# Experts in pairs of 512 tokens, the first layer in seven block products held in PSUM

## The chip, the cores and the metric

The kernel runs on one core of one Trainium2 chip. The metric is the device time of one execution in microseconds (us), and the figure of a kernel is the median of its runs. Engines are named as the profile names them: PE is TensorE's matrix multiplication and PEld its weight load, DVE is VectorE, ACT is ScalarE, POOL is GpSimd, SP is SyncE, which issues most of the DMAs.

## The reference, cut to what matters

The first part mixes each sequence by a Fourier transform; the second sends every token to one of 8 experts, a two-layer network with a relu between.

```python
batch, seq, dim = (8, 2496, 256)
N, D, E, F = (19968, 256, 8, 1024)
...
    X = np.fft.rfft(x, axis=1)
    Yr = Xr @ w_r - Xi @ w_i + b_r
    Yi = Xr @ w_i + Xi @ w_r + b_i
    Yr = np.sign(Yr) * np.maximum(np.abs(Yr) - lam, 0.0)
    Yi = np.sign(Yi) * np.maximum(np.abs(Yi) - lam, 0.0)
    y = np.fft.irfft(Y, n=x.shape[1], axis=1)
...
    logits = x @ w_gate + modality_bias[modality_id]
    e_idx = np.argmax(logits, axis=1)
    gate_w = probs[np.arange(N), e_idx]
    for e in range(E):
        mask = e_idx == e
        h = np.maximum(x[mask] @ w1[e], 0.0)
        out[mask] = gate_w[mask, None] * (h @ w2[e])
```

The experts are very unevenly used: of the 19,968 tokens of these inputs 9,993 go to expert 2 and 9,756 to expert 6.

## The kernel before

**The attention part** (0 to 627 us of the trace) works through the 8 sequences one after the other. Each has a stage of transforms and mixing, a stage of inverse products (`zs`, line 358), and then a "pivot" stage of 22 steps `j` (lines 372 to 387), in which PE multiplies, ACT and DVE split each result in a high and a low part, and the finished tokens are scattered by POOL into the DRAM tensor `xs`, sorted by expert. Routing, and a table of token tiles per expert, are made beside it. At some of the steps `j` a `SplitWeights.step` takes one 128x512 block of the experts' weights, splits it in a high (ACT, line 1070) and a low part (DVE or POOL, line 1071) and writes both to the DRAM tensor `wsp`. The order of the instructions on PE, ACT, DVE and POOL is the order in which the code emits them; SP issues its DMAs in that order too and waits at each for what it needs.

**The expert part** (627 to 1510 us) runs 78 tiles of 256 tokens (`NF`, `T`), sorted by expert; the table says the first row and the expert of each. Every number is a high and a low fp32r part, and every product three matmuls (high x high, high x low, low x high). For a tile, `ffn` does:
- first layer (line 829): 48 matmuls of 128x256, in four PSUM banks of a pool of four (`mhps`), each bank two of the 8 blocks of 128 hidden columns. A bank is then read twice: ACT writes `hh` = relu, 128x512 (line 831), DVE the low part `hl` (line 832);
- second layer (line 859): 48 matmuls into one bank `y` (two halves of 128 tokens x 256), all of them after the tile's first layer;
- output: half 0 is multiplied by the gate on ACT (line 851), half 1 on DVE (line 849), and POOL writes each with an indirect DMA (`put`, line 872).

Between the second and the third bank of a tile `prep` makes the next tile ready: DVE transposes (line 803), ACT casts the high part (line 807), POOL subtracts the low part (line 808). The weights have two buffers. `load_w` (line 771) loads 2 MB for each layer and tile, and only if the expert has changed; the first layer's load for tile i+2 is issued in the middle of tile i, the second layer's behind tile i. `load_x` (line 789) is issued four tiles ahead, in 8 DMAs of 32 KB and a small one for gates and indices. Between groups of matmuls `tick` lets the last sequence's routing, the second table and the scatters go on; `pack` and `half` compute the few tokens of the small remainders.

The code works only with blocks as they are stored: a weight `w1` of an expert is 256 x 1024, two blocks of 128 rows.

## Time and profile before

| | us |
|---|---|
| median of 3 runs (range) | 1517.15 (1514.96 to 1519.22) |
| profiled execution, device time | 1518.66 |
| its span in the trace | 1516.9 |
| PE busy | 1455.8 (96%) |
| DVE busy | 720.6 (48%) |
| ACT busy | 648.1 (43%) |
| POOL busy | 499.8 (33%) |
| mean granted clock of PE | 0.985 of full speed |

All rows below are of this one profiled execution. A row of a timeline gives the start, the length (of a run of xcount like instructions), the engine, the line of the kernel and "out<-in"; in brackets stands how long the engine was idle before it and what released it. Matmuls overlap: the length of one contains a pipeline that the next one shares, so the rate is read from the distance of starts. The columns of a group are busy time in us, mean ns of one, idle time just before them, and what ended most of that.

### The profile page before, as it was taken

The page shows a single profiled execution, that of the slowest core. Times are in us where ns is not written, and L with a number is a line of the kernel's source. Part 1 is how long each engine was busy: PE and PEld are TensorE (multiplying, and loading weights), DVE is VectorE, ACT ScalarE, POOL GpSimd, SP SyncE. Part 2 cuts the span into 40 slices and gives each one's busy share as a digit, 9 for nine tenths or more (in the row PEclk, how much of TensorE's full clock was granted, in tenths as well). Part 3 has the DMA queues.
Part 4 walks back from the last instruction along what each step waited for, and adds up shares of the span by engine and source line. Part 5 has one row for each costly group of instructions (what it writes and reads, how often), then busy time and mean ns, then how long its engine had stood idle before and what let it go on. Part 6 is the DMA issues. An engine that isn't in the chain of part 4 may idle for free. (4 is left out here: it accounts for less than half of the span.)

```text
span 1516.9 us, 34943 instructions
## 1 busy us (share of the span) xinstructions
PE 1455.8 (96%) x12378; PEld 1400.1 (92%) x12378; DVE 720.6 (48%) x1553; ACT 648.1 (43%) x1360; POOL 499.8 (33%) x501
## 2 busy tenths in 40 slices
PE   4799999999999988999999999999999999899998
PEld 2699999999999887999999999999999999899998
DVE  3667767677676664554333333333333333233332
ACT  3367677776767553532323323322322333232322
POOL 0001344444444453333643232222322323223222
PEclk8899999999999998999999999999999999999999
DMA  7858787979786655422442255642522227525520
GB/s 200 260 149 271 219 292 232 309 222 310 230 290 207 209 186 144 159 47 56 98 121 52 52 134 146 224 128 44 170 43 45 54 46 265 158 51 161 161 43 30
DMA packets 289702, 235.80 MB, mean 155 GB/s; under 512 B 208304, under 2 KB 243452, under 8 KB 285785
## 3 DMA queue, kind: packets, MB, share of 16 engines
q1 hardware_dynamic: 270677, 191.95, 44.4%
q0 software_dynamic: 18848, 41.58, 8.3%
q8 instruction: 100, 1.64, 0.5%
q14 instruction: 77, 0.63, 0.1%
HBM read 424.05 MB, written 99.68 MB: 345 GB/s over the span
## 5 line engine op out<-in xcount | busy, mean ns | idle before, releaser
L859 PE MATMUL y<-w,hh 128*128 128x256 f32 x2496 | 434.5, 277 | 1.1 <-ACT hh L831 1.0
L829 PE MATMUL h<-xh,w 128*128 128x256 f32 x2496 | 400.4, 277 | 4.3 <-DMA w<-wsp 3.3
L859 PEld LDWEIGHTS y<-w,hh 128*128 128x128 f32 x2496 | 377.4, 188 | 3.6 <-issue 1.7
L859 PE MATMUL y<-w,hl 128*128 128x256 f32 x1248 | 347.1, 278 | 0.6 <-DVE hl L832 0.4
L829 PEld LDWEIGHTS h<-xh,w 128*128 128x128 f32 x2496 | 337.3, 188 | 5.1 <-issue 3.9
L832 DVE SCALAR_TENSOR_TENSOR hl<-h,hh 128x512 fp32r<-128x512 f32 x312 | 209.2, 689 | 228.7 <-ACT hh L831 185.5
L872 POOL DMA_INDIRECT out<-o,ix x157 | 154.8, 986 | 419.2 <-ACT o L851 386.1
L829 PE MATMUL h<-xl,w 128*128 128x256 f32 x1248 | 244.2, 277 | 0.0
L831 ACT ACTIVATE hh<-h 128x512 fp32r<-128x512 f32 x312 | 178.1, 596 | 147.0 <-PE h L829 128.1
L859 PEld LDWEIGHTS y<-w,hl 128*128 128x128 f32 x1248 | 234.2, 188 | 2.0 <-DVE hl L832 1.7
L849 DVE TENSOR_SCALAR o<-y,xt 128x256 f32<-128x256 f32 x78 | 37.7, 484 | 328.3 <-ACT o L851 324.2
L829 PEld LDWEIGHTS h<-xl,w 128*128 128x128 f32 x1248 | 188.5, 188 | 0.2 <-DVE xl L808 0.2
L851 ACT ACTIVATE o<-y,xt 128x256 f32<-128x256 f32 x78 | 37.1, 476 | 351.5 <-PE y L859 351.5
L808 POOL TENSOR_TENSOR xl<-tr,xh 128x512 fp32r<-128x512 f32 x76 | 98.5, 1296 | 181.8 <-ACT xh L807 181.8
L547 POOL DMA_INDIRECT xs<-x1b,si x88 | 88.2, 1002 | 84.2 <-ACT ph L377 31.3
L372 PE MATMUL pv<-pv,z 128*120 128x136 f32 x704 | 111.8, 284 | 1.6 <-DVE mid L454 0.9
L547 POOL DMA_INDIRECT xs<-x,si x88 | 88.0, 1000 | 69.1 <-ACT ph L377 28.8
L334 PE MATMUL mx<-wmix,Xh 128*128 128x256 f32 x640 | 105.5, 288 | 3.5 <-DVE mx L327 3.1
L372 PEld LDWEIGHTS pv<-pv,z 128*120 128x120 f32 x704 | 100.1, 187 | 8.4 <-ACT z L362 2.2
L378 DVE TENSOR_TENSOR pl<-pv,ph 120x264 fp32r<-120x264 f32 x176 | 75.8, 431 | 64.4 <-ACT ph L377 52.2
L807 ACT CAST xh<-tr 128x512 fp32r<-128x512 f32 x78 | 48.4, 621 | 107.3 <-DVE ix L810 86.4
L303 PE MATMUL s<-c_m,a 128*128 128x128 f32 x640 | 86.1, 278 | 7.7 <-DMA a<-scr 7.7
(211 smaller groups left out, 2023.6 us busy)
## 6 DMA issues: line engine op xcount, KB each, us to landing
w<-wsp SPq DMA_DIRECT2D x156, 2048.0 KB
a<-scr SPq DMA_DIRECT2D x80, 256.0 KB
xt<-xs SPq DMA_DIRECT2D x624, 32.0 KB
wr<-in_moe_w SPq DMA_DIRECT2D x64, 256.0 KB
wsp<-wh SPq DMA_DIRECT2D x64, 256.0 KB
wsp<-wl SPq DMA_DIRECT2D x64, 256.0 KB
scr<-ev SPq DMA_DIRECT2D x98, 160.0 KB
x<-in_x SPq DMA_DIRECT2D x96, 156.0 KB
```

The lines of the kernel that those rows point to most:

```text
L303: nc.tensor.matmul(ps[:, c, :, i, :], at[:, i, c * 128:(c + 1) * 128], self.m[:, k1 * 128:(k1 + 1) * 128].rearrange("p (r k) -> p r k", r= ...
L334: self.nc.tensor.matmul(ps[:, i, :], t[:, c, 1 - i, :], self.w[:, i, c, lo, :], start=False, stop=n == len(ops) - 1, skip_group_check=True)
L372: nc.tensor.matmul(ps[:PK, c * 128:c * 128 + D // 2 + E], self.z[:, o:o + 3, :, :].rearrange("p n k r -> p (n k r)"), self.pv[:, c, :], st ...
L378: nc.vector.tensor_sub(pl, ps[:PK, :GC], ph)
L547: i = self.nc.gpsimd.indirect_dma_start(out=self.xs, out_offset=bass.IndirectOffsetOnAxis(ap=si[:, k:k + 1], axis=0), in_=rows, in_offset= ...
L807: nc.scalar.copy(xh, tr)
L808: (nc.gpsimd if i > 1 else nc.vector).tensor_sub(xl, tr, xh)
L829: nc.tensor.matmul(ps[:, q, :], w1[:, lo, c, f * 128:(f + 1) * 128], x[:, c, :], start=n == 0, stop=n == 5)
L831: nc.scalar.activation(hh[:, 2 * p:2 * p + 2, :], ps, AF.Relu)
L832: nc.vector.scalar_tensor_tensor(hl[:, 2 * p:2 * p + 2, :], ps, 0.0, hh[:, 2 * p:2 * p + 2, :], ALU.max, ALU.subtract)
L859: nc.tensor.matmul(y[s], lhsT, w2[:, lo, f, :], start=n == 0, stop=n == 23)
L872: ins = self.nc.gpsimd.indirect_dma_start(out=self.out, out_offset=bass.IndirectOffsetOnAxis(ap=ix, axis=0), in_=o, in_offset=None, bounds ...
```

## The change

**Units and pairs.** The table now gives first 32 pairs of 512 tokens (`PAIRS`, `T2`), then 14 single tiles of 256 (46 `SLOTS`). Each is done in four units U = 4i + f; unit f makes the 128 hidden columns f of each half of the 1024 hidden ones. `second(U - 2)` is a generator with the second layer of the unit two back, and pieces of it are emitted between the products of unit U. `y` takes two banks for a pair, one for each 256 tokens, and is added up over the four units.

**Seven products.** In pairs 7 to 31 (`LEAD` is 7) a unit has the form 2x2 blocks times 2x2 blocks: two 128-row blocks of x by two groups of 256 tokens, and two row blocks by two hidden halves of `w1`. Eight block products become seven, each of 3 matmuls of 128x256, with sums and differences of blocks. The sums of weights are the new `w3` (1.5 MB per expert, loaded by `load_s`), the sums of x the new `df`. Three PSUM banks hold the running block sums r1, r5 and r2: ACT copies r1 to the bank of r2 (both in PSUM), copies r5 and r2 to `s5` and `su2` in SBUF, and PE goes on adding to r1, r2 and r5 meanwhile; DVE adds them into `d`, a bank of the routing pool. Pairs 0 to 6 and the singles (`plain`) take eight products as before.

**Weights.** In the attention part `sum` adds two blocks of `w1` before they are split, at step j two before the `step` that writes them; a `step` now writes one DMA of 512 KB instead of two of 256 KB. In the expert part `combos`, advanced by each `tick` from unit 4 on, reads `w1` again, makes the three sums per expert, splits them and writes them to the DRAM tensor `wss` (8 MB read, 12 MB written).

**The rest.** x is loaded two slots ahead in 8 DMAs of 64 KB per pair. In pairs 7 to 31 all four output multiplications are on ACT. `pack` and `half` move behind the pairs, into the singles.

```diff
+T2 = 2 * T
+EARLY = -(-(NTOK - 2 * SEQ - E * (T2 - 1)) // T2)
+PAIRS = -(-(NTOK - E * (T2 - 1)) // T2)
+SLOTS = PAIRS + NF - 2 * PAIRS
+LEAD = 7
...
+        def low_parts():
+            if two:
+                split(0, b[0])
+                split(T, tr[:, 1, :])
+                yield
+                split(3 * T, df[:, 0, :])
+                yield
+                split(5 * T, df[:, 1, :])
+                return
...
+        if two:
+            V.tensor_sub(d[0], b[1], b[0])
+            V.tensor_sub(d[1], b[3], b[1])
+            yield
+            V.tensor_sub(d[2], b[3], d[0])
+            V.tensor_sub(d[3], b[2], d[2])
...
+    def plain(self, U, i, f, second):
+
+        n = self.size(i)
+        if n == T:
+            ps = self.bank().tile([128, 2, T], F32, tag="h", name=f"h_{U}")
+            for q, parts in enumerate((((0, 0), (1, n)), ((3, 0), (2, 2 * n)))):
+                self.mm(ps[:, q, :], self.terms(i, parts, f, 0, T))
+                next(second, None)
+                self.tick()
+            self.drain(U, slice(0, 2), slice(0, T), ps)
+            return
+        for q, parts in enumerate((((0, 0), (1, n)), ((3, 0), (2, 2 * n)))):
+            ps = self.bank().tile([128, T2], F32, tag="h", name=f"h_{U}_{q}")
+            for t in range(0, n, T):
+                self.mm(ps[:, t:t + T], self.terms(i, parts, f, t, T))
+            self.drain(U, q, slice(0, n), ps[:, :n])
+            for _ in range(2):
+                self.tick()
+                next(second, None)
+
+    def strassen(self, U, i, f, second):
+
+        nc, V = self.nc, self.nc.vector
+        xh, xl = self.xs[i][:2]
+        w1, w3, fs = self.wb[i % 2][0], self.w3[i % 2], slice(f * 128, (f + 1) * 128)
+        r1, r5, r2 = (self.hps[n].tile([128, T2], F32, tag="h", name=f"r{k}_{U}")[:, T:]
+                      for n, k in enumerate((1, 5, 2)))
+
+        def prod(ps, w, k, o, start):
+            o = slice(o * T, (o + 1) * T)
+            self.mm(ps, [(w[:, k, lo, fs], x[:, o]) for lo, x in ((0, xh), (0, xl), (1, xh))], start)
+
+        tmp = lambda tag: self.sp.tile([128, T], F32, tag=tag, name=f"{tag}_{U}")
+        a, b = slice(0, T), slice(T, T2)
+        s5, su2 = tmp("s5"), tmp("su2")
+        d = self.rt.ps.tile([128, 2, T], F32, tag="r", name=f"d_{U}")
+        hh, hl = self.hs[U]
+        next(self.next, None)
+        prod(r1, w1, 0, 0, True)
+        nc.scalar.copy(r2, r1)
+        prod(r5, w1, 3, 3, True)
+        nc.scalar.copy(s5, r5)
+        next(second, None)
+        prod(r2, w3, 0, 5, False)
+        nc.scalar.copy(su2, r2)
+        prod(r1, w1, 1, 1, False)
+        self.drain(U, 0, a, r1)
+        if f:
+            next(self.splits, None)
+        next(second, None)
+        self.tick()
+        prod(r2, w3, 1, 4, False)
+        V.tensor_add(d[:, 1, :], r2, s5)
+        prod(r5, w3, 2, 2, False)
+        V.tensor_add(d[:, 0, :], r5, su2)
+        self.drain(U, slice(0, 2), b, d)
+        next(second, None)
+        self.tick()
+        prod(r2, w1, 2, 6, False)
+        self.drain(U, 1, a, r2)
+        next(second, None)
+
...
+    def second(self, U):
...
+                c = 4 * q + f
+                a, l = hh[:, q, s * 128:(s + 1) * 128], hl[:, q, s * 128:(s + 1) * 128]
+                for x, lo in ((a, 0), (a, 1), (l, 0)):
+                    nc.tensor.matmul(y, x, w2[:, c // 2, lo, c % 2, :], start=f == 0 and k == 0 and s % 2 == 0,
+                                     stop=f == 3 and k == 5, skip_group_check=True)
+                    k += 1
+            if f == 3 and s % 2:
+                o = self.op.tile([128, 2, D], F32, tag="o", name=f"o_{i}_{s}")
+                for h in range(2):
+                    gate = g[:, s - 1 + h, 0:1]
+                    if h and not LEAD <= i < PAIRS:
+                        nc.vector.tensor_scalar_mul(o[:, h, :], self.y[i][s // 2][:, h, :], gate)
+                    else:
+                        nc.scalar.mul(o[:, h, :], self.y[i][s // 2][:, h, :], gate)
+                    self.put(ix[:, s - 1 + h:s + h], o[:, h, :])
+            yield
...
+        load(0)
+        for e in range(E):
+            load(e + 1)
+            yield
+            raw = raws.pop(e)
+            a11, a21, a12, a22 = (raw[:, c, h * 512:(h + 1) * 512] for c in range(2) for h in range(2))
+            V.tensor_add(a22, a21, a22)
+            yield
+            V.tensor_sub(a21, a11, a21)
+            yield
+            V.tensor_sub(a22, a22, a11)
+            yield
+            V.tensor_sub(a12, a12, a22)
+            yield
+            for k, a in enumerate((a22, a21, a12)):
+                w = wp.tile([128, 2, 512], F32R, tag="wt", name=f"ws_{e}_{k}")
+                nc.scalar.copy(w[:, 0, :], a)
+                V.tensor_sub(w[:, 1, :], a, w[:, 0, :])
+                nc.sync.dma_start(self.wss[e * 128:(e + 1) * 128, k * 1024:(k + 1) * 1024],
+                                  w.rearrange("p h f -> p (h f)").bitcast(F32))
+                yield
...
+        with ExitStack() as lead:
+            self.blocks(range(4))
+            self.more = self.combos(lead)
+            self.blocks(range(4, 4 * LEAD - 4))
+            for _ in self.more:
+                pass
+        with ExitStack() as mid:
+            w3 = self.pool("mw3", 1, mid)
+            self.w3 = [w3.tile([128, 3, 2, 512], F32R, name=f"w3_{i}") for i in range(2)]
+            self.sp = self.pool("mst", 1, mid)
+            for i in (LEAD, LEAD + 1):
+                self.load_s(i)
+            self.blocks(range(4 * LEAD - 4, 4 * PAIRS))
...
+        for U in units:
+            i, f = divmod(U, 4)
+            second = self.second(U - 2) if U >= 2 else iter(())
+            if i < SLOTS:
+                self.hs[U] = tuple(self.hp.tile([128, 2, T2], F32R, tag=t, name=f"{t}_{U}") for t in ("hh", "hl"))
+                if f == 0:
+                    self.next = self.prep(i + 1) if i + 1 < SLOTS else iter(())
+                if LEAD <= i < PAIRS:
+                    self.strassen(U, i, f, second)
+                else:
+                    next(self.next, None)
+                    self.plain(U, i, f, second)
+                    if f:
+                        next(self.splits, None)
...
+                            self.load_s(i + 2)
+            for _ in second:
+                pass
+            if f == 1 and 0 < i < SLOTS - 1:
+                self.load_w(i + 1, 1)
...
+    def sum(self, eng):
+
+        if self.raw and self.raw[0][1] == 1:
+            raw = self.raw[0][2]
+            for h in range(2):
+                eng.tensor_add(raw, raw, self.last[:, h, :])
...
+                    at_j = (3, 8, 13, 18) if b in (0, nb - 2) else (4, 10, 15)
+                    if j + 2 in at_j:
+                        sw.sum(nc.vector)
+                    if j in at_j:
                         sw.step(nc.vector)
```

PE, tile 39 of before, start of its second bank (`h_39_1`): one run of 12 matmuls, with a wait on PE's own record of the bank, and so for each bank.

```order
L829 MATMUL h_39_1_14800<-xh_39_14657,w1_1_8497 128x256 [waits PE_49]
L829 MATMUL h_39_1_14800<-xh_39_14657,w1_1_8497 128x256
L829 MATMUL h_39_1_14800<-xl_39_14658,w1_1_8497 128x256 x2
L829 MATMUL h_39_1_14800<-xh_39_14657,w1_1_8497 128x256 x4
L829 MATMUL h_39_1_14800<-xl_39_14658,w1_1_8497 128x256 x2
L829 MATMUL h_39_1_14800<-xh_39_14657,w1_1_8497 128x256 x2
```

PE, unit 29 (second unit of pair 7) of after: `r5` and `r2` are two of its running sums, `w1_1` and `w3_1` the weights and their sums, `y_6_0` an output bank of pair 6.

```order
L899 MATMUL r5_29_10890<-xh_7_10496,w1_1_8403 128x256 [waits DVE_49]
L899 MATMUL r5_29_10890<-xl_7_10497,w1_1_8403 128x256
L899 MATMUL r5_29_10890<-xh_7_10496,w1_1_8403 128x256
L983 MATMUL y_6_0_10664<-w2_0_8368,hh_27_10742 128x256 x2
L983 MATMUL y_6_0_10664<-w2_0_8368,hl_27_10743 128x256
L983 MATMUL y_6_0_10664<-w2_0_8368,hh_27_10742 128x256 x2
L983 MATMUL y_6_0_10664<-w2_0_8368,hl_27_10743 128x256
L899 MATMUL r2_29_10891<-xh_7_10496,w3_1_10462 128x256 [waits Activation_49]
L899 MATMUL r2_29_10891<-xl_7_10497,w3_1_10462 128x256
L899 MATMUL r2_29_10891<-xh_7_10496,w3_1_10462 128x256
L899 MATMUL r1_29_10889<-xh_7_10496,w1_1_8403 128x256
```

Between r1 and the first addition onto r2 now stand r5's three matmuls and six of the second layer, and that addition waits for ACT.

ACT, tile 3 of before: four relus, one cast for the next tile, one output multiplication.

```order
L831 ACTIVATE hh_3_9113<-h_3_0_9115 128x512 [waits PE_49,Activation_49]
L831 ACTIVATE hh_3_9113<-h_3_1_9132 128x512 [waits PE_49]
L807 CAST xh_4_9151<-tr_4_9149 128x512 [waits DVE_49]
L831 ACTIVATE hh_3_9113<-h_3_2_9157 128x512 [waits PE_49]
L831 ACTIVATE hh_3_9113<-h_3_3_9173 128x512 [waits PE_49]
L851 ACTIVATE o_3_9197<-y_3_9196,xt_3_8572 128x256 [waits DMAHW3_49,PE_49]
L831 ACTIVATE hh_4_9276<-h_4_0_9278 128x512 [waits PE_49,Activation_49]
```

ACT, unit 61 of after (the second unit of pair 15), with the outputs `o_14` of the pair before and the casts `xh_16` of the pair behind.

```order
L944 COPY r2_61_13443<-r1_61_13441 128x256 [waits PE_49]
L946 COPY s5_61_13444<-r5_61_13442 128x256 [waits PE_49,Activation_49]
L949 COPY su2_61_13445<-r2_61_13443 128x256 [waits PE_49,Activation_49]
L894 ACTIVATE hh_61_13439<-r1_61_13441 128x256 [waits PE_49]
L850 CAST xh_16_13381<-tr_16_13361 128x256 [waits Pool_49]
L850 CAST xh_16_13381<-tr_16_13361 128x512
L993 ACTIVATE o_14_1_13482<-y_14_0_13227,g_14_12095 128x256 [waits DMASW3_49,DMAHW4_49,DMASW2_49,PE_49]
L993 ACTIVATE o_14_1_13482<-y_14_0_13227,g_14_12095 128x256
L894 ACTIVATE hh_61_13439<-d_61_13446 128x2x256 [waits DVE_49]
L894 ACTIVATE hh_61_13439<-r2_61_13443 128x256 [waits PE_49]
L993 ACTIVATE o_14_3_13518<-y_14_1_13228,g_14_12095 128x256 [waits DMASW5_49,DMASW4_49,PE_49]
L993 ACTIVATE o_14_3_13518<-y_14_1_13228,g_14_12095 128x256
```

The copies, which didn't exist, stand ahead of the relus, and two casts and four multiplications stand between them and the next unit's copy `r2_62<-r1_62`.

DVE, pivot stage of the first sequence, before: `pl` is the low part that the next inverse product takes, `x1l` a split for a later sequence, line 1071 a weight split.

```order
L378 TENSOR_TENSOR pl_0_7_1184<-pv_0_7_1180,ph_0_7_1183 120x264 [waits PE_49,Activation_49]
L251 TENSOR_TENSOR x1l_2_9_1188<-x_2_4_842,x1h_2_9_1187 117x512 [waits Activation_49]
L378 TENSOR_TENSOR pl_0_8_1208<-pv_0_8_1204,ph_0_8_1207 120x264 [waits PE_49,Activation_49]
L387 COPY x1b_108<-i1_0_6_1211 117x264
L1071 TENSOR_TENSOR wl_0_1_1217<-wr_0_1_959,wh_0_1_1216 128x512 [waits Activation_49]
L378 TENSOR_TENSOR pl_0_9_1228<-pv_0_9_1224,ph_0_9_1227 120x264 [waits PE_49,Activation_49]
```

DVE, the same stage, after.

```order
L384 TENSOR_TENSOR pl_0_6_1171<-pv_0_6_1167,ph_0_6_1170 120x264 [waits PE_49,Activation_49]
L393 COPY x1b_109<-i1_0_4_1174 117x264
L1276 TENSOR_TENSOR wr_0_1_960<-wr_0_1_960,wt_0_3_1119 128x512
L1276 TENSOR_TENSOR wr_0_1_960<-wr_0_1_960,wt_0_3_1119 128x512 [waits DVE_49]
L384 TENSOR_TENSOR pl_0_7_1185<-pv_0_7_1181,ph_0_7_1184 120x264 [waits PE_49,Activation_49]
L257 TENSOR_TENSOR x1l_2_9_1189<-x_2_4_843,x1h_2_9_1188 117x512 [waits Activation_49]
```

Between two of the `pl` (line 378 before, 384 after) stand two additions onto the raw weight block `wr_0_1`, the second of which waits for the first.

## Rows read from the trace of the kernel before

**Rows 1.** The page's engine totals: busy us, share of the span, instructions.

```profile
PE 1455.8 (96%) x12378; PEld 1400.1 (92%) x12378; DVE 720.6 (48%) x1553; ACT 648.1 (43%) x1360; POOL 499.8 (33%) x501
```

**Rows 2.** Expert stage: length, busy of PE, PEld, DVE, ACT, POOL, clock, DMA.

```profile
627.20:1509.80 882.60, 877.25 (x7646) 868.79 (x7646) 314.40 (x643) 261.79 (x479) 275.65 (x256) 1.00 0.40 105
```

**Rows 3.** Groups by line, both layers: busy, mean ns, idle before, releasers.

```profile
L829 PE MATMUL h<-xh,w 128*128 128x256 f32 x2496 | 400.4, 277 | 4.3 <-DMA w<-wsp 3.3 <-ACT xh L807 1.0
L859 PE MATMUL y<-w,hh 128*128 128x256 f32 x2496 | 434.5, 277 | 1.1 <-ACT hh L831 1.0 <-DMA w<-wsp 0.2
```

**Rows 4.** TensorE's timeline where six tiles begin: start, us, instruction, [idle, releaser].

```profile
627.22 0.62 PE L829 MATMUL h<-xh,w 128*128 128x256 f32 x3 [0.99 <-ACT xh L807]
...
662.60 0.40 PE L829 MATMUL h<-xh,w 128*128 128x256 f32 x2
...
673.91 0.40 PE L829 MATMUL h<-xh,w 128*128 128x256 f32 x2
...
797.68 0.40 PE L829 MATMUL h<-xh,w 128*128 128x256 f32 x2
...
1208.84 0.39 PE L829 MATMUL h<-xh,w 128*128 128x256 f32 x2
...
1219.72 0.40 PE L829 MATMUL h<-xh,w 128*128 128x256 f32 x2
```

**Rows 5.** TensorE's timeline where weights came late.

```profile
1300.27 0.47 PE L829 MATMUL h<-xh,w 128*128 128x256 f32 x2 [3.32 <-DMA w<-wsp]
1300.59 0.40 PE L829 MATMUL h<-xl,w 128*128 128x256 f32 x2
...
1306.95 0.47 PE L859 MATMUL y<-w,hh 128*128 128x256 f32 x2 [0.98 <-ACT hh L831]
```

**Rows 6.** Timelines of PE and ACT, then groups: PSUM reads of 256 and 512.

```profile
1208.72 0.28 PE L859 MATMUL y<-w,hl 128*128 128x256 f32 x1
...
1209.04 0.48 ACT L851 ACTIVATE o<-y,xt 128x256 f32<-128x256 f32 x1 [4.59 <-PE y L859]
...
612.53 0.38 ACT L387 COPY x<-i 117x264 f32<-117x264 f32 x1
612.80 0.40 ACT L377 CAST ph<-pv 120x264 fp32r<-120x264 f32 x1
...
L319 ACT COPY mx<-bias 128x256 f32<-128x256 f32 x80 | 30.4, 385 | 1.5 <-DVE s L342 1.5
L327 DVE TENSOR_TENSOR mx<-mx,bias 128x256 f32<-128x256 f32 x80 | 31.8, 425 | 5.5 <-PE mx L326 4.7
L831 ACT ACTIVATE hh<-h 128x512 fp32r<-128x512 f32 x312 | 178.1, 596 | 147.0 <-PE h L829 128.1 <-issue 15.5 <-ACT o L851 3.4
L807 ACT CAST xh<-tr 128x512 fp32r<-128x512 f32 x78 | 48.4, 621 | 107.3 <-DVE ix L810 86.4 <-DVE tr L803 12.7 <-issue 8.2
```

**Rows 7.** Pivot stage: timelines of PE and DVE.

```profile
256.83 0.35 PE L384 MATMUL i<-ph,c_g 120*117 120x264 f32 x1 [0.35 <-DVE x1b L387]
...
263.21 0.68 DVE L1071 TENSOR_TENSOR wl<-wr,wh 128x512 fp32r<-128x512 f32 x1
```

**Rows 8.** Last batch's z products: timelines of PE and SyncE, and a window.

```profile
591.51 2.98 PE L358 MATMUL zs<-c_q,s 64*128 64x128 f32 x47
...
598.52 0.41 PE L358 MATMUL zs<-c_q,s 64*128 64x128 f32 x2 [0.97 <-issue]
...
604.27 3.05 PE L372 MATMUL pv<-pv,z 128*120 128x136 f32 x12 [0.88 <-DVE mid L454]
...
595.58 4.66 SPq L789 DMA_DIRECT2D xt<-xs  x6
...
600.00:605.00 5.00, 2.45 (x9) 1.64 (x9) 1.62 (x5) 1.31 (x2) 1.49 (x3) 0.50 0.36 73
```

**Rows 9.** The end: timelines of PE and GpSimd.

```profile
1509.51 0.28 PE L859 MATMUL y<-w,hl 128*128 128x256 f32 x1
...
1510.59 0.97 POOL L872 DMA_INDIRECT out<-o,ix  x1 [1.76 <-DVE o L849]
```

More of the change, by code (lines that the diff above doesn't have):

```diff
@@ L619, in cumsum, with clamp @@
         self.sums = t
+    def clamp(self, out, t, buf, limit):
+        V = self.nc.vector
+        yield from self.cumsum(t, buf, E)
+        cum = self.sums
+        V.tensor_scalar_min(cum, cum, float(limit))
+        yield
+        V.tensor_copy(out[:, :1], cum[:, :1])
+        V.tensor_sub(out[:, 1:], cum[:, 1:], cum[:, :E - 1])
+        yield
     def tiles_early(self):
@@ L692, in table @@
             yield
-            if n > E:
-                V.memset(one[:, 2 * E:2 * E + 1], 0.0)
-                V.memset(one[:, 3 * E + 1:3 * E + 2], 0.0)
+            for o in fill:
+                V.memset(one[:, o:o + 1], 0.0)
+            if fill:
                 yield
@@ new lines, in size, with expert, regs, load_w @@
+    def size(self, i):
+        return T2 if i < PAIRS else T if i < SLOTS else TH
+    def expert(self, i):
+        e = self.reg(i, 1, E - 1)
+        return e, dict(cond=self.reg(i, 2, 1), cond_hint=False) if 2 <= i < SLOTS else {}
+    def regs(self, i):
+        if i not in self.ws:
+            self.ws[i] = self.expert(i)
+        return self.ws[i]
+    def load_w(self, i, layer, to=None):
+        e, kw = self.regs(i)
+        row = self.wsp[bass.ds(e * 128, 128), layer * 4096:(layer + 1) * 4096]
+        w = self.wb[i % 2][layer] if to is None else to
+        o = "p a b f -> p (a b f)" if layer == 0 else "p a b c f -> p (a b c f)"
+        return self.nc.sync.dma_start(w.rearrange(o).bitcast(F32), row, **kw)
@@ L988, in tick @@
         next(self.late, None)
+        next(self.more, None)
     def run(self, late):
@@ new lines, in run @@
+        for _ in self.splits:
+            pass
[4 more added lines that the diff above has]
+            for _ in self.more:
+                pass
+        with ExitStack() as mid:
[5 more added lines that the diff above has]
+            self.blocks(range(4 * LEAD - 4, 4 * PAIRS))
@@ new lines, in run @@
+        with ExitStack() as tail:
+            self.hw = self.pool("mhw", 1, tail)
+            self.pool("mhpad", 1, tail).tile([128, 48], F32, name="mhpd")
+            self.hf = self.pool("mhf", 1, tail)
+            self.hx = self.pool("mhx", 1, tail)
+            self.blocks(range(4 * PAIRS, 4 * SLOTS + 2))
+            for _ in self.side:
+                pass
+            k = SIDE + HALF
+            more = self.nc.values_load(self.rt.ti[k:k + 1, 3:4], min_val=0, max_val=1,
+                                       skip_runtime_bounds_check_because="a flag")
+            with self.tc.If(more > 0):
+                for i in range(k, SIDE + E):
+                    self.load_half(i)
+                    for _ in self.half(i):
+                        pass
@@ L1027, in run @@
-        for _ in self.side:
-            pass
-        k = SIDE + HALF
-        more = self.nc.values_load(self.rt.ti[k:k + 1, 3:4], min_val=0, max_val=1,
-                                   skip_runtime_bounds_check_because="a flag")
-        with self.tc.If(more > 0):
-            for i in range(k, SIDE + E):
-                self.load_half(i)
-                for _ in self.half(i):
-                    pass
+            if at in (44, 45, 49, 53):
+                next(self.side, None)
 class SplitWeights:
```

463 lines of the change are left out of this document (230 added, 233 removed).

## The prediction

> **What bounds the kernel now.** I read the engine totals first: TensorE is busy 96% of the span, the next engine 48% [rows 1]. Totals mix stages, so the windows come next [rows 2]: in the expert stage (627.2 to 1509.8, 58% of the span) TensorE works 877.25 of 882.60 us at granted clock 1.00, VectorE 314, ScalarE 262. There the time is the number of matmuls times their pitch, and nothing else. The groups of the first layer say the same from the other side: its 3744 matmuls waited 4.3 us in all, 3.3 of these for a weight DMA, and the second layer is not late either [rows 3]. A matmul's "277 ns" is a modelled end; the pitch has to come from starts. One undisturbed tile begins at 1208.84 and the next at 1219.72 [rows 4]: 10.88 us for 96 matmuls, **113.4 ns each**. There is a second pace: the tile from 662.60 to 673.91 took 11.31 us, 117.8 ns each, without a wait of its own, and 15 tiles from 627.22 to 797.68 took 170.46 us where 15 at the fast pace take 163.2 [rows 4]. The one real stall stands at 1300.27, where the weights of a third expert change in a row arrive late (3.32 us, and 0.98 more at 1306.95) [rows 5].
>
> **What it removes.** The second layer keeps its matmuls. In the first layer a unit (128 columns of each hidden half, 512 tokens) needs 8 block products of 3 matmuls; the seven products need 21. That runs in pairs 7 to 31, so 25 pairs of 4 units: 100 x 3 = **300 matmuls fewer** of 7488, all 128x256 as before. 300 x 0.1134 = **-34.0 us**, if the pitch stays and nothing new ends last. This term is simple; the rest of the working asks how much of it is handed back.
>
> **The new chain inside a unit.** Before, a tile's PSUM results were only read, long before the bank was wanted again. Now TensorE adds onto a bank that ScalarE has just filled, a few matmuls later. I lay out one unit of 45 matmuls (5.10 us) from the first matmul of r1. From the start of the last matmul that writes a bank to ScalarE's start on it takes 1209.04 - 1208.72 = 0.32 us [rows 6]. A 256-wide ScalarE copy out of PSUM took 0.385 us, a VectorE add of that size 0.425 [rows 6]; copies that follow each other directly start 0.27 apart [rows 6].
> - r1's third matmul starts at 0.23, the copy r2 <- r1 runs 0.55 to 0.93; r2's first matmul, the 13th, is due at 1.36 and its weights one pitch earlier, 1.25. Slack 0.3 us.
> - r2's third matmul starts at 1.59, su2 is ready at about 2.30; r2 is added to again at 2.72 (weights 2.61). Slack 0.3.
> - r2 again at 2.95, VectorE's d add ends 3.73; the last product is due at 4.08 (3.97). Slack 0.24.
>
> So three of the four units of a pair should cost nothing, but by margins of two to three pitches. The second unit of each pair differs: ScalarE there also has two splits (0.62 for 512 columns) and all four output multiplications (0.48 each) [rows 6], which before it shared with VectorE. Queued behind them is the next unit's copy r2 <- r1: I get 6.43 for its end against 6.35 wanted, about 0.1 us late, plus a restart of about the same (after the stall at 1300.27 the next matmul starts 0.32 us later for two matmuls, where 0.23 is normal [rows 5]). 0.2 x 25 = **+5 us**, bounds 0 (it just makes it) and 10 (0.4 each). No row of before shows a PSUM to PSUM copy on ScalarE; the bounds of its length are the 256-wide copy to SBUF (0.385) and the 512-wide ScalarE pass (0.596) [rows 6]. I take the first, since the number of elements is the same. The break-even is 34 / 100 = 0.34 us lost per unit.
>
> VectorE and GpSimd have room: per unit VectorE gets two adds and three instead of two drains, some 2.4 us of 5.1, and per pair 3 us of transposes and differences; GpSimd some 8 us of 20.4. I cost them at nothing.
>
> **First pairs and singles.** There the second layer now follows two units behind the first instead of one tile half, so no relu is waited for at the start; in the early tiles 7.3 us were lost against the fast pace (170.46 - 163.2). I take back **-3** (0 to -7), since the combination work (8 MB read, 12 MB written, with VectorE and ScalarE passes) comes into these same pairs. The first prep is longer: the first matmul waited 0.99 us for a cast of one tile [rows 4]; now twice the tokens and the differences of x stand ahead of it: **+1**.
>
> **Sums in the attention part.** In the pivot stage VectorE now adds two 128x512 blocks twice per expert, 8 calls of 2 x 0.68 us [rows 7] = 1.36 each, the second waiting on the first. Queued behind them are the VectorE passes that the next pivot product needs. One split of that length at such a place already made TensorE wait 0.35 at 256.83; one at 263.21 cost nothing [rows 7]. With twice that length I take 0.5 us each, **+4** (0 to 11, the whole length).
>
> **The last batch's z products.** 47 of them ran in 2.98 us from 591.51, and the other 17 came in ones and twos with up to 1 us of "issue" between, while SyncE issued the x loads; the next stage began at 604.27, and the clock granted fell to 0.50 in 600 to 605 [rows 8]. At the first pace the 64 take 4.1 us instead of 12.8: 8.7 us were lost there. Four tiles' loads (32 DMAs of 32 KB) become two pairs' (16 of 64 KB), the same bytes. I take a third back: **-3** (-9 to +3).
>
> **Weight switches.** With these inputs nearly all tokens go to two experts; the leftovers make singles of other experts that stand in a row at slots 32 to 35, four switches behind each other where there were three. A single gives its weights 10.9 us of lead. The 4.3 us of [rows 5] may become 1 to 10: **+1** (-4 to +6). Inside the pairs a switch moves 5.5 MB per 20.4 us, before it was 4 MB per 10.9, so I add nothing there.
>
> **The end.** After the last matmul (1509.51) one output and one put remained, 1510.59 [rows 9]; now both halves of the last two are multiplied and put behind it: **+1**.
>
> **Sum**, on the profiled execution: 1518.66 - 34.0 + 5 - 3 + 1 + 4 - 3 + 1 + 1 = 1490.7, call it **1491**. The median of before is 1.5 below that execution, so a median after may read 1489; I leave 1491.
>
> **The rivals.**
> - *The slow pace holds.* If the many short waits on ScalarE leave TensorE at 117.8 ns through the 100 units, 4500 x 4.4 ns = +20: **1511**. For it: the pace changed at a disturbance and lasted for many tiles [rows 4]. Against: the fast pace came back and held. 0.17.
> - *Copies and adds late in every unit*: the slower outcome. If the copy within PSUM, and the relays from r2 to su2 and d, take 0.45 us more than the rows show (the 512-wide price and a longer release), two products per unit stall 0.15 and restart 0.1: 0.5 x 100 = +50 in place of the +5, **1536**. It decides at 0.34 us per unit, some 0.37 more in each link. The margins of 0.24 to 0.3 speak against it, narrowly. 0.07.
> - *The clock falls in the units.* At the lower level (1.2 GHz, granted 0.50) a matmul costs double: 4500 x 0.1134 = +510, about **2000**. Here the clock fell where TensorE worked less than half of the time for some us [rows 8], and the expert stage kept 1.00 with the stall of 3.3 us in it [rows 2, 5]. 0.01. The Trainium skill, "TensorE: Matmul & The Clock Gate", section "A second HAM failure mode: psum-queue depth-cycling", describes a kernel whose cycling through PSUM banks idled TensorE briefly between groups until its clock swung between the two levels; by that rule the units are its place. No run here shows it yet.
> - *Sums, combinations and switches weigh more*, each near its upper end: +9 to +16, **1500 to 1507**. 0.09.
> - *More is gained* at the z stage and in the early tiles: **1478 to 1484**. 0.06.
> - *It doesn't do what it says* (the units run as plain ones): no gain, about **1519**. The order of instructions shows 21 matmuls per unit, so 0.01.
>
> The forecast itself, 1481 to 1500, has 0.59.
>
> **How the numbers follow.** 1481 to 1511 holds the forecast (0.59), the heavier sums (0.09) and most of the slow pace (0.13): 0.81. A measurement can tell about 0.3%, 4.6 us, from no change: faster is below 1512.6. The forecast, the heavy sums, the extra gain and most of the slow pace are there: 0.86. Slow pace with heavy terms, or no change: 0.06. Late copies in every unit and the clock: 0.08.
>
> **What would show it.** First-layer matmuls of the expert stage down by 300 (the count), and a pair in 20.4 us (pace: 21.2). TensorE waiting on ScalarE's r copy once per pair, at its third unit, for 0.1 to 0.2 us; on any other product, and more than 0.34 per unit, the late copies are right. VectorE's two adds ahead of a wait of TensorE of about 0.5 in the pivot stage. The z products of the last batch closer together. DMA waits only at slots 32 to 35. If the pitch outside the units changes too, the term that failed is the pace, not the chain.

## The result: 1.0% slower

The changed kernel takes 1533.23 us in the median of 4 runs (1526.63 to 1535.98), the kernel before 1516.18 beside it; the ratio is **1.0103 [1.0067, 1.0139]**. The forecast was 1491, with a range that ended at 1511. The profiled execution has a span of 1531.3 us against 1516.9.

The page of the changed kernel, engine totals and the two groups that answer to [rows 1, 3]:

```profile
PE 1440.5 (94%) x12078; PEld 1381.5 (90%) x12078; DVE 897.0 (59%) x2005; ACT 815.8 (53%) x1920; POOL 577.4 (38%) x582
...
L983 PE MATMUL y<-w,hh 128*128 128x256 f32 x2496 | 462.3, 279 | 15.7 <-DMA w<-wsp 14.6
...
L899 PE MATMUL r<-xh,w 128*128 128x256 f32 x1400 | 316.1, 284 | 12.7 <-DVE d L957 8.1
```

300 matmuls are gone, as the change promises, and TensorE is busy 15 us less. But it is no longer 99% busy in the expert part: both layers now wait (15.7 us for weights, 12.7 mostly for VectorE's `d`), where they waited 1.1 and 4.3 before. The windows of the expert part (pairs 0 to 6, pairs 7 to 31, the singles; columns as in [rows 2]) show where:

```profile
623.20:781.00 157.80, 153.63 (x1303) 151.53 (x1303) 118.92 (x265) 63.69 (x119) 75.39 (x65) 1.00 0.81 247
781.00:1326.00 545.00, 532.34 (x4500) 528.36 (x4499) 297.10 (x673) 308.98 (x797) 215.93 (x200) 1.00 0.44 123
1326.00:1521.90 195.90, 180.99 (x1548) 174.37 (x1546) 63.16 (x131) 57.03 (x124) 60.15 (x71) 0.97 0.54 166
```

Idle PE time in a window hides a slower pitch, so I also made a sum from the starts of all matmuls of the two layers: their number at 113.4 ns; other matmuls in between; distances over 135 ns, less 113.4 (waits); and what is left (slower pitch).

| us, first to last matmul of the layers | before | changed |
|---|---|---|
| matmuls x 0.1134 us | 849.0 | 819.1 |
| other matmuls between | 16.0 | 12.0 |
| waits | 10.0 | **46.0** |
| slower pitch | 7.3 | **21.4** |
| sum | 882.3 | 898.4 |

The first two rows save 34 us, as forecast (36 matmuls of a small remainder count in the first row now, in the second before). The waits cost 36 more and the pitch 14 more. Of the 46 us of waits 5.4 lie in pairs 0 to 6, **21.05 in pairs 7 to 31, of which 18.6 in the third unit of a pair**, and 19.5 in the singles, of which 14.9 are two waits for second-layer weights and 1.4 the matmuls just behind the longer one, about 213 ns apart at a lower clock. Outside, the expert part begins 4.0 us earlier (623.25) and its tail is 2.3 us longer. 16.1 - 4.0 + 2.3 is the 14.4 us of the two spans.

### The profile page after: what moved, and what is told of

It is laid out like the page before. It is cut to its first block, busy times and chain, and to the rows that moved or that the text cites. A ratio compares the mean times of both kernels' runs of the same rounds, so it can differ in the third digit from the quotient of the medians.

```text
span 1531.3 us, 34368 instructions
## 1 busy us (share of the span) xinstructions
PE 1440.5 (94%) x12078; PEld 1381.5 (90%) x12078; DVE 897.0 (59%) x2005; ACT 815.8 (53%) x1920; POOL 577.4 (38%) x582
## 5 line engine op out<-in xcount | busy, mean ns | idle before, releaser
L983 PE MATMUL y<-w,hh 128*128 128x256 f32 x2496 | 462.3, 279 | 15.7 <-DMA w<-wsp 14.6
L983 PEld LDWEIGHTS y<-w,hh 128*128 128x128 f32 x2496 | 382.1, 189 | 16.2 <-issue 14.9
L899 PE MATMUL r<-xh,w 128*128 128x256 f32 x1400 | 316.1, 284 | 12.7 <-DVE d L957 8.1
L899 PEld LDWEIGHTS r<-xh,w 128*128 128x128 f32 x1400 | 243.1, 189 | 16.7 <-DVE d L957 10.6
L899 PE MATMUL r<-xl,w 128*128 128x256 f32 x700 | 196.4, 281 | 0.0
L851 POOL TENSOR_TENSOR xl<-tr,xh 128x256 fp32r<-128x256 f32 (+1 forms) x88 | 83.8, 971 | 240.8 <-ACT xh L850 240.5
L899 PE MATMUL h<-xh,w 128*128 128x256 f32 x896 | 169.0, 282 | 0.0
L895 DVE SCALAR_TENSOR_TENSOR hl<-r,hh 128x256 fp32r<-128x256 f32 x200 | 84.1, 420 | 142.1 <-ACT hh L894 127.8
L894 ACT ACTIVATE hh<-h 128x512 fp32r<-128x512 f32 x112 | 66.8, 597 | 163.3 <-PE h L899 151.2
L895 DVE SCALAR_TENSOR_TENSOR hl<-h,hh 128x512 fp32r<-128x512 f32 x112 | 77.0, 688 | 122.4 <-ACT hh L894 105.2
L899 PEld LDWEIGHTS h<-xh,w 128*128 128x128 f32 x896 | 132.0, 189 | 2.7 <-issue 2.5
L899 PEld LDWEIGHTS r<-xl,w 128*128 128x128 f32 x700 | 132.0, 189 | 0.0
```

The lines of the kernel that those rows point to most:

```text
L851: low.tensor_sub(xl[:, o], src, xh[:, o])
L894: nc.scalar.activation(hh[:, q, o], ps, AF.Relu)
L895: nc.vector.scalar_tensor_tensor(hl[:, q, o], ps, 0.0, hh[:, q, o], ALU.max, ALU.subtract)
L899: self.nc.tensor.matmul(ps, w, x, start=start and k == 0, stop=k == len(ops) - 1, skip_group_check=True)
L983: nc.tensor.matmul(y, x, w2[:, c // 2, lo, c % 2, :], start=f == 0 and k == 0 and s % 2 == 0, stop=f == 3 and k == 5, skip_group_check=True)
```

## Where the third unit waits

Three timelines of the changed kernel in the third unit of pair 14: TensorE, VectorE, GpSimd.

```profile
947.20 0.40 PE L899 MATMUL r<-xh,w 128*128 128x256 f32 x2
...
948.26 0.28 PE L983 MATMUL y<-w,hl 128*128 128x256 f32 x1
950.27 0.39 PE L899 MATMUL r<-xh,w 128*128 128x256 f32 x1 [1.73 <-DVE d L957]
...
949.78 0.43 DVE L957 TENSOR_TENSOR d<-r,s 128x256 f32<-128x256 f32 x1 [1.36 <-remote]
...
944.09 0.99 POOL L998 DMA_INDIRECT out<-o,ix  x1
945.38 1.14 POOL L998 DMA_INDIRECT out<-o,ix  x1 [0.30 <-issue]
946.82 0.97 POOL L998 DMA_INDIRECT out<-o,ix  x1 [0.30 <-issue]
948.10 0.97 POOL L998 DMA_INDIRECT out<-o,ix  x1 [0.30 <-issue]
```

The last matmul onto r2 starts at 947.20. VectorE was free at 948.42, needs no more than that matmul, and begins its add only at 949.78. Nothing on VectorE's queue explains it, and the add's other input, s5, was copied between 945.35 and 945.74. The trace also records when each semaphore was raised: TensorE's update for this matmul, which ended at 947.48, and the one for the next product came at 949.76 and 949.81. I call an update late that comes over 30 ns after the end of its matmul. Of 752 updates by TensorE between 790 and 1330 us **98 are late**, mostly by 0.35 to 0.95 us and by up to 3.3, and they stand in the third units, where GpSimd issues the pair's four output writes (puts) behind each other. Updates by ScalarE and VectorE were never late. Theory PUTS: the puts hold TensorE's updates back. Rival QUEUE: the four multiplications, casts and differences make ScalarE and VectorE late themselves.

**e1_no_puts** takes the puts away and leaves the rest:

```diff
-                    self.put(ix[:, s - 1 + h:s + h], o[:, h, :])
+                    if not LEAD <= i < PAIRS:
+                        self.put(ix[:, s - 1 + h:s + h], o[:, h, :])
```

> Leaves out the indirect DMA writes of the outputs (puts) of pairs 7 to 31; the multiplications stay. In the changed kernel TensorE waits 21.05 us within these pairs, all in the third unit of a pair, where four puts run back to back on GpSimd and TensorE's semaphore updates reach ScalarE and VectorE up to 0.9 us late. Theory PUTS (the puts hold the updates back): the waits fall from 21 us to under 5, the time from 1533 to 1514-1518. Rival QUEUE (ScalarE's casts and four multiplications and VectorE's differences are simply late themselves): the waits stay near 21 us and the time at 1530 or more.

1518.14 us, ratio 1.0005 [0.9987, 1.0022]; waits in the pairs 3.8 us, late updates 4 of 773. Its group of first-layer matmuls:

```profile
L899 PE MATMUL r<-xh,w 128*128 128x256 f32 x1400 | 313.4, 282 | 1.5 <-issue 1.1 <-DVE d L957 0.4
```

QUEUE falls: the multiplications and casts are all there.

**e2_spread_puts** keeps the puts in a list and issues one behind each unit (the last one held is never issued):

```diff
+                    if LEAD <= i < PAIRS - 1:
+                        self.held.append((ix[:, s - 1 + h:s + h], o[:, h, :]))
...
+        if self.held:
+            self.put(*self.held.pop(0))
```

> All puts are kept, but in pairs 7 to 30 one is issued at the end of each unit instead of four behind each other. PUTS: a single put made updates only about 0.1 us late in the kernel before, inside the slack of 0.24 us, so the waits in the pairs fall from 21 to under 7 us and the time to 1515-1520. QUEUE: no change, 1530 or more. If only the number of puts counts and not their closeness, the waits stay at 21, moved to other units.

1521.17 us, 1.0015 [1.0003, 1.0028]; 10.5 us of waits, half of what was there and more than the 7 that I had expected. Nothing on GpSimd separates the third put from the fourth, so these two still ran together, and the first unit of the next pair waited 0.15 us in 22 pairs.

**e8_puts_only** ties each put to one of the four splits of a pair, which wait for ScalarE's casts and so lie apart:

```diff
             low.tensor_sub(xl[:, o], src, xh[:, o])
+            if self.held:
+                self.put(*self.held.pop(0))
```

> The four puts behind the four splits, without the 32 bytes. PUTS: waits in the pairs under 6 us, slow matmuls 20-21 us as in the changed kernel, 1515-1519. QUEUE (ScalarE and VectorE late themselves): 21 us of waits, 1530 or more.

1520.28 us, 1.0012 [0.9997, 1.0026]; 6.3 us of waits, 11 late updates of 754; time and waits lie a little above what I had expected. All puts are there, so it was their closeness that held the updates back.

**r1_changed_again** is the changed kernel unaltered. Several later runs fell on chips where the kernel before takes about 1493 us instead of 1517, and there no update was more than 60 ns late. I call such a chip prompt, the others late.

> The changed kernel itself, unaltered, on another chip. In the runs on some chips TensorE's semaphore updates were late behind puts (98 to 120 between 790 and 1330 us), in those on others none was, with the same puts; there the kernel before is 25 us faster too. Theory CHIP (the lateness belongs to a chip): on a prompt chip the changed kernel has no late update, under 4 us of waits in the pairs and a ratio of 1.005-1.008; on a late one 98-120 late updates, 21 us and 1.009-1.014. Rival LAYOUT (the new layout of the last runs ended the lateness): late updates and 21 us of waits here even where the kernel before runs in about 1492 us.

1499.98 against 1494.25 us, **1.0033 [1.0017, 1.0048]**; no late update of 754, 2.4 us of waits in the pairs. Timelines of its TensorE, VectorE and GpSimd at the same place of pair 14, where the four puts run as closely as before:

```profile
926.06 0.40 PE L899 MATMUL r<-xh,w 128*128 128x256 f32 x2
...
926.38 0.43 DVE L957 TENSOR_TENSOR d<-r,s 128x256 f32<-128x256 f32 x1 [0.20 <-PE r L899]
...
925.68 0.97 POOL L998 DMA_INDIRECT out<-o,ix  x1 [0.30 <-ACT su L949]
```

And its group of first-layer matmuls:

```profile
L899 PE MATMUL r<-xh,w 128*128 128x256 f32 x1400 | 313.6, 282 | 0.5 <-DVE d L957 0.4
```

From the last matmul's start to the add are 0.3 us, not 2.6. So the lateness goes with the chip: every run on chips 6, 12 and 15 has late updates, none on 0, 7 and 9 has one beyond 60 ns. Where it occurs, it stands beside puts that run close together. What differs between the chips, and how a put holds an update back, no run shows. The ratio was better than the 1.005 to 1.008 that I had expected.

## The waits for weights

Timelines of TensorE in slot 33 of the changed kernel and of SyncE's issues ahead of it:

```profile
1358.33 0.39 PE L899 MATMUL h<-xh,w 128*128 128x256 f32 x2
1371.82 0.77 PE L983 MATMUL y<-w,hh 128*128 128x256 f32 x2 [13.10 <-DMA w<-wsp]
...
1354.71 3.10 SPq L1098 DMA_DIRECT2D pw<-in_moe_w  x4
1358.19 1.83 SPq L802 DMA_DIRECT2D w<-wsp  x2
```

A window of the same kernel within the wait (columns as before):

```profile
1365.00:1370.00 5.00, 0.00 (x0) 0.00 (x0) 0.00 (x0) 0.00 (x0) 0.00 (x0) 0.50 1.01 428
```

The DMA engines are busy all the time (share 1.01, 428 GB/s) and 2 MB of the pack's weights (line 1098) were issued just ahead of the second layer's. **e6_align_puts** is e8 with 32 bytes ahead of all buffers (below), **e7_align_puts_pack** moves the pack's eight steps behind the four switches:

```diff
-            if at == 4:
+            if at == 16:
                 self.side = self.pack()
-            if at in (4, 11, 12, 20, 21, 22, 28, 36):
+            if at in (16, 22, 23, 30, 31, 32, 38, 44):
...
-            if at in (44, 45, 49, 53):
+            if at in (50, 51, 54, 57):
```

> The 32 bytes, and each of a pair's four puts stands behind one of GpSimd's four splits, so that no two run behind each other. PUTS: the waits in pairs 7 to 31 fall from 21 to under 6 us, with ALIGN 1500-1505; with PUTS alone 1515-1519; if neither holds, 1530 or more.

> As the run before, and the pack's loads (2 MB at a time) begin at slot 36 instead of 33, behind the four weight switches. If the 13.3 us wait for second-layer weights at 1358 comes from sharing bandwidth with the pack's first 2 MB, it falls to 6-9 us and the time by 4-7 against the run before; if the four switches alone need it, no change within 2.

e6: 1520.57, 1.0010 [1.0000, 1.0021], and a wait of 12.69 us in the same place of TensorE's timeline:

```profile
1360.10 0.77 PE L987 MATMUL y<-w,hh 128*128 128x256 f32 x2 [12.69 <-DMA w<-wsp]
```

e7: 1510.06, **0.9932 [0.9912, 0.9951]**, and its timeline there:

```profile
1363.47 0.74 PE L987 MATMUL y<-w,hh 128*128 128x256 f32 x2 [2.99 <-DMA w<-wsp]
```

9.7 us of the wait were the pack's share, more than the 4 to 7 that I had expected. **e7_again** repeats it on another chip:

> The best version so far (32 bytes, puts behind splits, pack behind the four switches; 0.993 of the kernel before on a chip whose updates come late), again, to see what it is worth on whatever chip comes. On a prompt chip the spread puts save nothing (2.4 us of waits were left in the pairs anyway) and the later pack about 10 us of the changed kernel's 1.0033: 0.996-0.998. On a late chip: 0.991-0.995.

1505.91 against 1514.39, **0.9951 [0.9935, 0.9967]**, on a chip with late updates (12 of 770). So on two late chips the corrected version is 0.5 to 0.7% faster than the kernel before, while the changed kernel had 1.0103 on the first chip and, with the 32 bytes (e5, below), 1.0125 on the chip of e7. On a prompt chip it was not run; its nearest relatives there (p2 and q1, below) take as long as the kernel before.

## What the seven products are worth by themselves, and the pitch

**e3_all_plain** runs all pairs with eight products; **e4_plain_one_piece** also puts the second layer's 24 matmuls of a unit in one piece:

```diff
-                if LEAD <= i < PAIRS:
-                    self.strassen(U, i, f, second)
-                else:
...
             for _ in range(2):
                 self.tick()
-                next(second, None)
+                if q:
+                    next(second, None)
+                    next(second, None)
```

> All 32 pairs run as plain ones (eight products, no copies within PSUM, no d adds); the second multiplication of an output goes back to VectorE, w3 is not loaded. 300 matmuls more: +34 us. The waits of 21 us in pairs 7 to 31 go, whatever their cause. Pace theory BOUNDARY (the slower pitch is entered where the first layer follows the second, two times per unit here): slow matmuls stay about half of all, and the time is 1533 + 34 - 21 - 3 = 1540-1546. Pace theory WAITS (the copies' waits make the pitch slow): the slow pitch goes as well, 1528-1534.

> As the run with all pairs plain, but the 24 second-layer matmuls of a unit stand in one piece behind its 24 of the first layer, so that the first layer follows the second once per 48 matmuls instead of twice. BOUNDARY: the slow matmuls fall from about half to a quarter or less, and 6 to 12 us are gained on the run before it. WAITS or any cause in the data: no difference beyond 2 us.

e3: 1546.89, 1.0192 [1.0168, 1.0215]; no wait in the pairs, but 19.7 us of slower pitch. Beside e1 on the same chip (1518.14) the seven products are worth 29 of the 34 us, once their waits are gone (e1 leaves out puts; against e2, which issues all but one, 26). So the slower pitch doesn't come from the copies' waits. e4: 1552.07, 1.0212 [1.0194, 1.0229], with 18.9 us of slower pitch and 10.5 us of waits in the first pairs (4.8 in e3). BOUNDARY in the form that I gave it falls: fewer steps from layer to layer, the same slow share. Three units of e4 begin in TensorE's timeline at

```profile
1001.92 0.40 PE L899 MATMUL h<-xh,w 128*128 128x256 f32 x2
...
1007.37 0.40 PE L899 MATMUL h<-xh,w 128*128 128x256 f32 x2
...
1013.03 0.40 PE L899 MATMUL h<-xh,w 128*128 128x256 f32 x2
```

so 48 matmuls take 5.45 us in one unit and 5.66 in the next. In e3, with the same buffers, runs of 24 alternate instead (113.9 and 118.0 ns). The pace turns at each return to the first layer, and half of the matmuls stay slow however seldom it turns: the order of the work counts.

In the changed kernel the two paces can be read off one unit:

```profile
1021.36 0.28 PE L899 MATMUL r<-xh,w 128*128 128x256 f32 x1
1021.48 0.28 PE L899 MATMUL r<-xl,w 128*128 128x256 f32 x1
1021.60 0.40 PE L899 MATMUL r<-xh,w 128*128 128x256 f32 x2
1021.84 0.28 PE L899 MATMUL r<-xl,w 128*128 128x256 f32 x1
...
1023.02 0.39 PE L899 MATMUL r<-xh,w 128*128 128x256 f32 x2
1023.25 0.28 PE L899 MATMUL r<-xl,w 128*128 128x256 f32 x1
1023.36 0.28 PE L899 MATMUL r<-xh,w 128*128 128x256 f32 x1
1023.48 0.39 PE L983 MATMUL y<-w,hh 128*128 128x256 f32 x2
```

By the exact starts four steps from 1021.36 take 0.474 us (118.5 ns each), four from 1023.02 take 0.454 (113.5). The pattern returns in every unit: about matmuls 1 to 13 and 25 to 37 slow, the others fast, and here too it turns wherever the first layer follows the second. The kernel before carries small unused tiles between its buffers, so I looked at addresses within a partition of SBUF.

**e5_align** puts 32 bytes ahead of all:

```diff
+        pool("mal", 1).tile([128, 8], F32, name="mald")
```

> One 32-byte tile is put ahead of the expert part's buffers in SBUF, nothing else. In the changed kernel all operands of the matmuls begin 32 bytes past a multiple of 64, and the pitch flips between 113 and 118 ns each time the first layer follows the second; in the kernel before every second tile's operands begin at a multiple of 64, and its pitch flips only for the first five matmuls of the other tiles. Theory ALIGN: with all of them on multiples of 64 the slow matmuls go; their 21.4 us over the expert part fall below 5, and the time to 1514-1519. Rival (the flips come from the order of the work or from waits): 21 us and 1530-1536 stay. The waits behind the puts (21 us) stay in either.

1537.84, 1.0125 [1.0108, 1.0142], 21.5 us of slower pitch, the same pattern: ALIGN falls. **p1_shift64** and **p2_shift128** move x and the hidden blocks against the first weight buffer (on e7 without the 32 bytes), **p3_before_shift** moves the second weight buffer of the kernel before:

```diff
-        pool("mqx", 1).tile([128, 16], F32, name="mqxd")
+        pool("mqx", 1).tile([128, 32], F32, name="mqxd")
...
-        pool("mp", 1).tile([128, 16], F32, name="mpad")
+        pool("mp", 1).tile([128, 32], F32, name="mpad")
```

> Built on the run with puts behind splits and the later pack, without the 32 bytes. x and the hidden blocks are moved by 64 bytes and the second weight buffer by as much, so that in even slots x and the weights begin at the same place modulo 128 (distance 64 so far); odd slots keep their distance. Theory DISTANCE (the pitch depends on where the two operands of a matmul lie to each other): even and odd slots now differ in their share of slow matmuls by half or more. Rival (addresses don't matter): 21-22 us of slow matmuls in all, even and odd slots alike, and about 1510.

> As before, with 128 bytes instead of 64: in even slots the distance of x from the weights turns from 192 to 64 modulo 256, odd slots keep it. DISTANCE modulo 256: even slots differ from odd ones. Rival: no difference, about 1510.

> The kernel before, with its second weight buffer moved by 64 bytes, so that in odd tiles x and the weights lie at the same place modulo 128. DISTANCE: odd tiles get slow stretches (10.9 us a tile becomes 11.1 to 11.3) and the time rises by 8-17 us. Rival: tiles stay at 10.9 us and the time within 3 us of 1517.

Each ran once, on a chip where the kernel before, also run once, took 1491.97; the slower pitch repeats well (19.9 to 22.0 us in the nine runs of the changed kernel's layout, the 32-byte shift included). p1: 1499.28, 35.0 us of slower pitch (22.0 in e7); p2: 1491.14, 25.3 us; p3: 1514.35, 28.4 us (7.3 in the kernel before, read on the first chip). In p1 and p2 even and odd slots are slowed alike (10.2 and 11.0 us of p1's in the pairs), so DISTANCE falls as I stated it, and p1's 35.0 us speak against its rival too. The first matmuls of three tiles in p3's timeline of TensorE:

```profile
951.74 0.40 PE L829 MATMUL h<-xh,w 128*128 128x256 f32 x2
...
963.04 0.40 PE L829 MATMUL h<-xh,w 128*128 128x256 f32 x2
...
974.44 0.28 PE L829 MATMUL h<-xh,w 128*128 128x256 f32 x1
```

11.30 and 11.40 us a tile, where [rows 4] have 10.88. So **64 bytes between two buffers cost the kernel before 21 us of pitch**: where the operands lie is shown to matter. Both kinds of tiles became slow, though only the odd ones' buffers moved, so the distance within a tile isn't the whole rule. What still differs is the distance at the step from one layer to the next; five layouts vary it (**q1_all_four** and, on the changed kernel, **q2_layout_only**; then **d96**, **d160** and **d128**, all but q2 with e8's puts and e7's later pack), by unused tiles between the buffers; these lines are from q1:

```diff
         wb = lambda p, i: (p.tile([128, 4, 2, 512], F32R, name=f"w1_{i}"),
-                           p.tile([128, 4, 2, 2, D], F32R, name=f"w2_{i}"))
+                           p.tile([128, 16], F32, name=f"w1pad_{i}"),
+                           p.tile([128, 4, 2, 2, D], F32R, name=f"w2_{i}"))[::2]
...
+        pool("mqh", 1).tile([128, 16], F32, name="mqhd")
         self.hp = pool("mh", 3)
```

> Puts behind splits and the later pack as before; new is the layout. All that streams through TensorE (x, and the second layer's weights) begins at 32 modulo 128 bytes, all that is loaded as its weights (the first layer's weights and their sums, the hidden blocks) at 96. In the changed kernel this distance of 64 holds within a layer, but at the step from one layer to the other the running stream and the next load lie at the same place modulo 128. Theory STEP (that coincidence flips the pitch): the slow matmuls fall from 22 us to under 6 us and the ratio to the kernel before from 0.993 to 0.980-0.985. Rival (only the distance within a layer counts): 20 us or more of slow matmuls, 0.992-0.995.

> The changed kernel with the new layout alone. STEP: slow matmuls from 21.4 us to under 6 us, the waits of 21 us in the pairs and of 15 us for weights stay; ratio to the kernel before from 1.010 to 0.997-1.002. Rival: 20 us or more, 1.009-1.013.

> Puts behind splits, later pack, and a layout in which the second layer's weights begin 96 bytes past the first's modulo 256 (0 so far), hidden blocks as much past x; within a layer the distances stay. In the kernel before the step from a tile's second layer to the next tile's first is by 96 or 160 too, since its two buffer sets lie apart, and there the pitch falls back to the fast level. Theory STEP96: slow matmuls from 22 us to under 8. Rival: 20 us or more in another pattern.

> The same with 160 bytes. STEP96 says under 8 us of slow matmuls; the rival 20 or more.

> The same with 128 bytes, which is 0 modulo 128 as in the changed kernel. If only the place modulo 128 counts, the pattern is that of the changed kernel (first 13 and middle 12 matmuls of a unit slow, 14 us in the pairs); if modulo 256, another one.

| | time | ratio | slower pitch, us |
|---|---|---|---|
| q1_all_four | 1492.79 | 0.9994 [0.9981, 1.0007] | 24.2 |
| q2_layout_only | 1503.69 | 1.0063 [1.0040, 1.0085] | 24.7 |
| d96_layout | 1493.24 | one run | 28.8 |
| d160_layout | 1494.44 | one run | 28.7 |
| d128_layout | 1501.19 | one run | 30.0 |

STEP and STEP96 fall. Each layout gives a pattern of its own (in q1 most of the first layer's matmuls at the start of a unit are fast and the second layer's slow), none reaches the 7 us of the kernel before. That the places of the buffers move the pitch is shown by p1 and p3, that the order of the work does, by e3 and e4. By which rule stays open, and so whether the new kernel is slow for its layout or for its order, and whether that order allows a fast layout at all.

## Why the prediction was wrong, point by point

- *The removal, -34.0*: right to the tenth in the sum of starts, and 29 us of it show in the time when the waits are out of the way (e1 against e3).
- *The chain in the unit*: right where the reading was done. The three slacks of 0.24 to 0.3 us hold on a prompt chip (r1: hardly a wait but one of 0.06 us at r2's first addition in the third unit, forecast 0.2). On the first chip **the failed step is "GpSimd ... I cost them at nothing"**: the four puts, laid behind each other, made updates by TensorE mostly 0.35 to 2 us late, and a chain with 0.24 us of slack passes that on. The term was +5, bounds 0 to 10; it measured 21.05. That the waits stand in the unit that was named is luck in part: the addition that was priced waited only 0.07 us, in 24 pairs; of the 18.6 us 12.2 stand before the unit's last product, in 13 pairs, and 4.8 before r2's second addition, in 5. [rows 6] gave the relay as 0.32 us from one undisturbed place. The trace of before had late updates, too (36 of its 58 late ones in the expert part beside a put, mostly by 0.1 us), without a chain to feel them.
- *The pace*: a rival with 0.17, at +20 for the pairs. It happened: 13.7 us in the pairs, 21.4 in all against 7.3, and in the singles too (4.4 against 0.4), the sign that the prediction gave for a failed pace. A pair took 21.8 us, 21.0 in r1, where 20.4 was forecast. The cause was not the one named (waits on ScalarE; e3 has none and the same pace). The forecast took 113.4 ns as TensorE's own; p3 shows that it held only for the layout that the change replaced, e3 and e4 that the order counts as well. Which of the two made the new kernel slow stays open.
- *Weight switches*: +1 (-4 to +6) measured +10.3 (14.9 against 4.6). I counted four switches and 10.9 us of lead, but not the pack's 2 MB, which the change moved right in between; moved away, 9.7 us came back (e7).
- *Sums in the attention part*: +4 measured +1.2 (the eight pivot stages took 188.9 us, now 190.1); no run took the sums out, but they cost little. *The z products*: -3 measured -6.3; the last batch's stage went from 36.8 to 30.6 us, though its end still waits; why it gained twice the forecast no run shows. With the start these make -4.0 where I had +2. The group of z products and, from the timeline of TensorE, that wait:

```profile
588.78 3.74 PE L364 MATMUL zs<-c_q,s 64*128 64x128 f32 x58
...
600.91 1.00 PE L378 MATMUL pv<-pv,z 128*120 128x136 f32 x3 [6.46 <-DVE mid L460]
```

- *First pairs, -3*: not seen; 5.4 us of waits and 3.3 of slower pitch there, in the same tiles before 2.6 and 3.4. *The end, +1*: +2.3.
- *The rivals*: the late chain in every unit did not come, three of four units run free; it came in one, for another reason. The clock stayed at 1.00 in the pairs. So the Trainium skill's case of a clock that swings with PSUM banks ("TensorE: Matmul & The Clock Gate", "A second HAM failure mode: psum-queue depth-cycling") is not this one.

What failed together were three terms that I had each taken near their good end: 16 for the puts, 14 for the pace and 9 for the weights are 39 of the 42 us between 1491 and 1533. The puts alone would not have saved it: on a prompt chip, without late updates, the change is still no gain (r1, 1.0033).

## What to carry to other kernels

When a change puts a short chain between engines into an inner loop, price the signal itself at the busiest place, with the DMA issues that run beside it, not at one quiet place; and lay indirect DMAs apart. A pitch read from the old kernel holds for the old buffers' places and the old order; unused tiles between its buffers are a hint that their places were chosen. And of work moved "to the end" every load counts where the weights already change quickly.

## What the hardware showed that I had not expected

- On some chips TensorE's semaphore updates come mostly 0.35 to 2 us late beside indirect DMAs that GpSimd issues closely; on others, with the same program, they don't (98 of 752 against 0 of 754). The same chips differ by 25 us in the kernel before, 22.6 of these by the time of the first expert matmul (627.22, and 604.60 in p3). That the late updates explain this too was not tried.
- A 64-byte move of one buffer changed TensorE's pitch from 113.4 to about 118 ns through most of the expert part (p3).
- In the 13 us wait the granted clock fell to 0.50, the lower level of 1.2 GHz, and the matmuls behind it started about 213 ns apart until 1374.7; after the stall of 3.3 us in [rows 5] it had stayed at 1.00.
